# A Nyström attention and MLP kernel: 64x32 products for C·v, ScalarE's squares for the row deviations, landmark sums exchanged by DMA, and a new order of work

## The chip, the cores and the metric

The kernel runs on one core of one Trainium2 chip. The metric is the device time of one execution in microseconds, as the median of several runs. Beside it stands one profiled execution, from which all durations of parts are taken; its own time is told by its span, from the first to the last instruction.

## What is computed

Inputs q, k, v are (8 batches, 8 heads, 576 rows, 64 columns). For each batch and head the rows are averaged in 32 groups of 18 into landmarks, three softmaxes are formed, one 32x32 matrix is inverted by six steps of an iteration, and the product goes, batch by batch, into a layer norm and a two-layer MLP with a residual.

```python
q_lm = q.reshape(B, H, 32, 18, D).mean(axis=3)      # k_lm alike
A = sm(q, k_lm); Bm = sm(q_lm, k_lm); C = sm(q_lm, k)
Z = Bm^T / (norm1(Bm) * norminf(Bm) + 1e-6)
for _ in range(6): Z = 2 * Z - Z @ Bm @ Z
x = (A @ Z @ C @ v)  as rows of 512 = 8 heads x 64
out = x + relu(layernorm(x) * g @ w1) @ w2          # w1 512x2048, w2 2048x512
```

## The kernel before

**Units and sets.** A unit is four heads of one batch, so that a batch has two units. Batch 0 goes first by a path of its own; batches 1, (2, 3), (4, 5), (6, 7) are the sets 0 to 3 of `def_set`, and in a set of four units the units go in pairs y = 0, 1. The name of a tile ends in the set and the pair or unit.

**An order written out.** Every step is declared with `op(name, engines, tiles, function)`. The string `ORDER` lists all steps by number with the letter of the engine that does each (P TensorE, D VectorE, A ScalarE, G GpSimd, S the SyncE queue, which only issues DMAs). Each engine works through its own steps strictly in that order; across engines only the data decide. A tile takes the first free slot of its kind (`slots`, lines 297 to 305), and waits for the slot's last reader.

**Landmark sums** (lines 694 to 763). The rows of a head lie nine to a partition, so that the 18 rows of a landmark are two neighbouring groups of nine, in two places of the transposed unit `xT`. For k VectorE reduces `xT` (`add_`, two reductions of 128x576 per unit, 24 in all); for q GpSimd adds the nine rows in four steps (`asum_`), VectorE transposes and reduces the small rest (`sT_`, `sR_`). Both leave in `part` the sums of one half of the heads' landmarks on one block of 32 partitions and of the other half on the next block. `spread` (line 796) is two matmuls with the constant matrix `spread16`, which bring both halves to all blocks in PSUM (`psp`), and `lm` (line 802) copies them to SBUF. From `lm` come three products: `psb` (scores of landmarks with landmarks), `psec` (landmarks of q with k) and `psea` (landmarks of k with q).

**Tile places.** TensorE's array is used in parts where the operands are small: `tile_position=(rb, cb)` gives the first row and column of the part. `psb`, `psec`, `psea` and the iteration use 32x32 parts, of which 16 exist; `psec` as written uses eight (its column place is `32 * ((p_ + 2 * (w % 2)) % 4)`, the same for r = 0 and r = 1), `psea` all sixteen. `product` (line 876), C times v, uses 64x64 parts: 18 groups of four matmuls for a pair of products, each with 64 landmarks of two heads and 130 columns, which are v's columns and a column of ones of both heads. Half of what it gives is one head's landmarks with the other head's v, and is not used.

**v's load.** `load_into` (line 320) brings a unit of v by one DMA, `load_swapped` (line 323) by three, since the heads then have to lie in other partitions.

**Layer norm and MLP.** `rows` makes 128 rows of x in PSUM (`psy`), `x_` copies them to SBUF on ScalarE or VectorE (line 983), `measure` (line 996) takes mean and variance on VectorE by bn_stats and bn_aggr, 36 times, and `rstd` turns five or four blocks' variances into 1/deviation on ScalarE. `psm`, `psh`, `relu` (ScalarE and VectorE) make the hidden layer; `pso` or, for batches 2 to 7, the seven products `ps7a`, `ps7c`, `ps7e` of `def_seven` with its `hmix` sums (GpSimd and VectorE) the second; results are added to x on VectorE and stored by DMAs from SP and ScalarE.

Of the kernel before, what the change touches and what calls it, by code (L numbers as in the profile page):

```python
# [10 lines left out]
FP32 = mybir.dt.float32  # L11
UINT32 = mybir.dt.uint32
# [4 lines left out]
P = 128  # L17

ORDER = """
0G 20P 23P 4S 12P 14P 24P 17P 11P 2S 1S 3S 6S 7S 10P 21P 28G 38P 25A 26D 34P 39D 40P 29P 30A 31P 27D  # L20
37P 32P 42D 41D 18P 33D 43P 65P 44A 45D 66A 61P 67P 46P 47P 250G 48D 22P 19P 15P 62A 68A 69A 71D
245G 49P 50D 63P 35P 13P 79G 80D 51P 52D 64A 36A 81P 70D 53P 72P 73A 5S 95S 54D 8P 9D 105A 106G 55P
56D 57P 74P 82D 260P 83D 58D 16P 84D 96S 59P 75A 76A 60D 85P 251D 86D 89P 90D 87P 88D 126P 261A 262D
108G 77G 94S 103G 93S 97S 101G 91D 92D 78D 107A 102G 127P 128P 129P 130A 167P 141P 142A 252P 253A
145P 169D 104A 168D 98S 254D 149P 150D 147P 148A 172P 173A 176P 247P 177A 248A 259D 255D 174P 175A
246D 256P 257A 146A 170P 171D 109G 110G 121P 122P 123P 111G 124P 268P 156P 258D 151D 249D 267P 112A
125A 275A 269A 270A 271A 157D 277A 158D 131P 132P 133P 134P 178P 163P 278D 279D 117G 273A 433G 274A
99S 113G 135A 180D 263S 164A 159P 280P 281D 160A 165P 166A 114G 264A 100S 115G 116G 265S 118G 136P
137P 266G 161P 179D 429G 119G 138P 139P 162D 282P 283D 140A 181P 182A 183P 284P 276D 285A 143P 187P
184D 286P 144A 188A 272D 152D 185P 186A 287D 297P 298D 299D 189P 191D 190D 288P 289A 294P 290P 295A  # L30
201P 202P 296A 300P 301A 291D 292P 293A 120G 455G 212P 213P 435G 436G 437G 310P 438G 445G 302A 303G
308P 309A 214P 330P 434D 444D 312D 311D 313D 332D 192P 193A 153D 154D 198P 199A 155A 441D 430D 439D
431D 331D 442D 440D 432D 443D 234P 556D 215P 304P 235P 236P 305A 306A 196P 446G 447G 203P 204P 194P
195A 237P 238P 205P 206P 451G 197A 307G 314P 315A 337P 339P 448G 449D 822G 338A 555D 239P 240P 241P
322P 207P 208P 574D 565D 569G 450D 340A 323A 216P 242D 209D 210S 217P 324D 341P 343D 223P 335P 244S
336A 342D 333P 463D 218P 219P 577G 452D 220D 344P 352P 353D 467G 468G 469G 470G 334A 826G 348P 345A
349A 346P 347A 457G 318P 319A 224P 316P 317A 225P 226P 227P 481P 458G 465D 459G 460G 482A 350P 454D
354D 357P 471D 464D 472D 351A 453D 363P 228P 229P 364D 358A 361P 230P 362A 461D 462D 365D 493P 494A
359P 368P 360A 483P 495P 355P 325D 326D 505A 369A 356A 231D 233A 200G 374P 375P 366P 367A 370P 371A
573G 506D 456D 507P 508P 509D 320P 321D 385P 484P 486A 487A 489A 510P 834D 511D 466D 491A 386P 387P  # L40
485A 388P 211S 512P 376P 473S 474G 490A 377P 496P 498A 501A 499A 497A 513D 514P 327D 488D 492D 328D
396P 397P 475S 476G 566G 828G 829G 830G 831G 572G 477S 478G 838G 839G 844G 564G 568G 503A 378P 379P
380P 515D 823D 502A 221S 504D 372P 516P 479S 480A 500D 517D 836D 528P 529P 530D 531D 398P 399P 373A
# [57 lines left out]
1496D 1521D 1427D 1523P 1524P 1525P 1421S 1526P 1428A 1516G 1515G 1522D 1529P 1530P 1429A 1531P  # L101
1532P 1527D 1528D 1539P 1540P 1564P 1541P 1542P 1168S 1533D 1535S 1418A 1536D 1537A 1538S 1543D
1534S 1545S 1432A 1546D 1548A 1547A 1549P 1565P 1550P 1566P 1551P 1567P 1568D 1569S 1570S 1552P
1553P 1554P 1555P 1544A 1556P 1557D 1558A 1559S
"""


# [1156 lines left out]
```

## Time and profile before

| what | value |
|---|---|
| median of 3 runs (lowest, highest) | 260.67 us (260.29, 261.9) |
| span of the profiled execution | 258.5 us |
| TensorE busy | 249.9 us, 97% of the span, 3499 matmuls |
| VectorE busy | 212.3 us, 82%, 472 instructions |
| ScalarE busy | 163.9 us, 63%, 304 instructions |
| GpSimd busy | 177.5 us, 69%, 180 instructions |
| DMA | 36.3 MB, mean 140 GB/s |

The profile names an instruction by its line, engine, operation and tiles, written out<-in with buffer numbers left out. PE is TensorE's matmul, PEld its weight load, DVE VectorE, ACT ScalarE, POOL GpSimd, SP the queue that issues DMAs; a trailing q marks an engine's sequencer. Matmuls overlap one another, so the mean duration of one is longer than the time it adds; the chain of waits cuts the time into pieces without overlap and is the better scale for a group. In the chain's rows stand the start, the length, the engine with the output tile, and xN, the number of instructions of the piece.

### The profile page before, as it was taken

What the parts mean: (1) busy time and instruction counts of PE and PEld (TensorE: products, weight loads), DVE (VectorE), ACT (ScalarE), POOL (GpSimd) and SP (SyncE); (2) the same over time, 40 slices, a digit from 0 to 9 for tenths busy, and PEclk for the clock granted to TensorE, in tenths of its full rate; (3) what the DMA queues carried; (4) which work ended last, traced back from release to release, by engine and by line L of the source; (5) the groups of instructions that cost most, each with busy time, mean ns of one, the idle gap of its engine ahead of it and who ended that gap; (6) DMA issues with size and microseconds to landing.
All of it is one profiled execution on the core that took longest, in us unless ns stands there. A gap on an engine that the chain in (4) does not pass through costs nothing.

```text
span 258.5 us, 8351 instructions
## 1 busy us (share of the span) xinstructions
PE 249.9 (97%) x3499; PEld 179.8 (70%) x3499; DVE 212.3 (82%) x472; ACT 163.9 (63%) x304; POOL 177.5 (69%) x180
## 2 busy tenths in 40 slices
PE   7898999999999999999999999999999999999993
PEld 7766465556554557777766787777867787788981
DVE  1669899999999989997998869898547999878661
ACT  1588886747766999778756997868666245644000
POOL 8324899689794789699999995782078505966600
PEclk9999999999999999999999999999999999999999
DMA  6999999999749176949704832500130100510356
GB/s 234 367 269 338 374 210 208 207 235 244 227 127 178 29 164 87 221 89 286 140 4 121 231 93 61 127 3 3 41 85 0 44 20 9 115 23 20 82 121 184
DMA packets 23277, 36.32 MB, mean 140 GB/s; under 512 B 2116, under 2 KB 11592, under 8 KB 23240
## 3 DMA queue, kind: packets, MB, share of 16 engines
q1 hardware_dynamic: 12456, 23.37, 29.6%
q0 software_dynamic: 9504, 10.36, 25.1%
q10 hardware_dynamic: 1280, 2.07, 3.1%
q8 instruction: 27, 0.44, 0.7%
q14 instruction: 10, 0.08, 0.1%
HBM read 36.70 MB, written 9.44 MB: 178 GB/s over the span
## 4 chain that ended last, share of the span: by engine, by line
PE 85%; DMA 7%; ACT 3%; DVE 2%; issue 1%; SPq 1%; ACTq 0%; DVEq 0%
PE psh L193 23%; PE ps7a L193 16%; PE pso L193 15%; PE ps7c L193 8%; DMA w1s<-in_moe_w_ch_dram 5%; PE ps7e L193 4%; PE psm L193 3%; PE psy L193 3%; DMA stg_q<-in_q_dram 3%; PE it L193 2%; PE pscv L193 2%; PE psd L193 1%; PE psec L193 1%; PE psea L193 1%; PE pso_74a L193 1%
## 5 line engine op out<-in xcount | busy, mean ns | idle before, releaser
L203 ACT ACTIVATE hT<-psh 128x576 f16<-128x576 f32 x106 | 65.8, 650 | 30.4 <-PE psh L193 28.6
L193 PEld LDWEIGHTS <-hT 128*128 128x128 f16 x688 | 64.6, 98 | 22.6 <-issue 3.1
L193 PE MATMUL psh<-ea,m 128*128 128x288 f16 x512 | 78.2, 286 | 0.1
L193 PEld LDWEIGHTS <-m 128*128 128x128 f16 x512 | 48.9, 98 | 15.6 <-issue 1.3
L193 PE MATMUL pso<-w,hT 128*128 128x512 f16 x176 | 45.5, 380 | 0.0
L207 POOL TENSOR_TENSOR mix<-hT 128x1024 f16<-128x1024 f16 x8 | 17.0, 2125 | 27.4 <-ACT hT L203 27.4
L210 DVE SCALAR_TENSOR_TENSOR x<-ps7a,rstd,x 128x256 f32<-128x256 f32 x48 | 21.3, 477 | 6.7 <-PE ps7a L193 4.9
L193 PE MATMUL ps7a<-mix,hT 128*128 128x256 f16 x192 | 25.9, 273 | 0.0
L1068 DVE TENSOR_SCALAR hT<-psh 128x576 f16<-128x576 f32 x22 | 16.4, 753 | 10.1 <-PE psh L193 9.9
L997 DVE BATCH_NORM_STATS2 six<-x 128x6 f32<-128x512 f32 x36 | 24.2, 673 | 0.0
L207 POOL TENSOR_TENSOR ea<-ea,lns 128x576 f16<-128x576 f16 (+1 forms) x14 | 17.7, 1261 | 7.2 <-ACT lns L203 4.0
L200 ACT CAST m<-psm 128x512 f16<-128x512 f32 (+1 forms) x25 | 19.1, 793 | 4.5 <-PE psm L193 3.4
L200 ACT COPY x<-psy 128x512 f32<-128x512 f32 (+1 forms) x29 | 16.8, 587 | 7.6 <-PE psy L193 7.2
L193 PEld LDWEIGHTS <-mix 128*128 128x128 f16 x192 | 18.2, 98 | 4.3 <-issue 1.5
L207 POOL TENSOR_TENSOR mix<-mix,hT 128x1024 f16<-128x1024 f16 x8 | 16.9, 2124 | 6.2 <-DVE mix L207 5.8
L207 POOL TENSOR_TENSOR hT<-hT 128x1024 f16<-128x1024 f16 x9 | 19.1, 2123 | 0.2
L207 POOL TENSOR_TENSOR hT<-hT,mix 128x1024 f16<-128x1024 f16 x7 | 15.1, 2166 | 4.4 <-PE ps7e L193 2.5
L214 DVE TENSOR_REDUCE part<-xT_k 128x32 f16<-128x576 f16 x24 | 17.1, 737 | 0.0
L207 POOL TENSOR_TENSOR asum_q<-asum_q 128x256 f32<-128x256 f32 (+1 forms) x24 | 15.1, 628 | 1.5
L203 ACT ACTIVATE ec<-psec 128x256 f16<-128x256 f32 (+1 forms) x42 | 12.4, 428 | 5.3 <-PE psec L193 5.3
L193 PE MATMUL psy<-zcbd,ea 128*128 128x256 f16 x80 | 14.8, 273 | 0.2 <-ACT x L200 0.2
L200 POOL CAST natv<-stg_v 128x1152 f16<-128x1152 f32 (+1 forms) x12 | 13.8, 1163 | 1.4 <-DMA stg_v<-in_v_dram 1.3
(174 smaller groups left out, 471.2 us busy)
## 6 DMA issues: line engine op xcount, KB each, us to landing
out_dram<-x SPq DMA_DIRECT2D x55, 128.0 KB, 2.7
stg_v<-in_v_dram SPq DMA_DIRECT2D x10, 576.0 KB, 5.1
w1s<-in_moe_w_ch_dram SPq DMA_DIRECT2D x8, 512.0 KB, 11.6
nat_q<-in_q_dram POOLq DMA_DIRECT2D x7, 576.0 KB, 8.7
nat_k<-in_k_dram POOLq DMA_DIRECT2D x7, 576.0 KB, 7.5
w<-in_moe_w_ch_dram POOLq DMA_DIRECT2D x4, 512.0 KB, 8.5
out_dram<-x ACTq DMA_DIRECT2D x15, 128.0 KB, 2.4
stg_v<-in_v_dram SPq DMA_DIRECT2D x6, 288.0 KB, 4.5
```

The source lines that it names most:

```text
L193: keep(nc.tensor.matmul(o, l, r, start=start, stop=stop, tile_position=(rb, cb), skip_group_check=(skip or cb != 0)))
L200: keep(nc.scalar.copy(o, i) if e == "A" else ENGINES[e].tensor_copy(out=o, in_=i))
L203: keep(nc.scalar.activation(*args, **kw))
L207: keep(ENGINES[e].tensor_tensor(out=o, in0=a, in1=b, op=f))
L210: keep(ENGINES[e].scalar_tensor_tensor(out=o, in0=a, scalar=s, in1=b, op0=f0, op1=f1))
L214: keep(nc.vector.tensor_reduce(out=o, in_=i, axis=axis, op=f))
L997: keep(nc.vector.bn_stats(out=T(f"six_{j}")[:], in_=T(f"x_{j}")[:]))
L1068: keep(nc.vector.tensor_scalar(out=o, in0=T(psh)[:, :, 0:HS], scalar1=0.0, scalar2=None, op0=ALU.max))
```

## The change

Six things change together.

1. **64x32 products.** `product` makes, instead of one matmul with 64 landmarks and 130 columns, two with 32 landmarks and 65 columns of their own head's v. There are twice as many matmuls (288 become 576), in eight places of 64x32; the results and what reads them (`cv`) are half as wide.
2. **ScalarE's squares.** `x_` also gives the row sum (`accum_out`), and `measure` becomes one ScalarE Square of 128x512 per block, with the row sum as bias and the sum of squares as a second output. bn_stats and bn_aggr go.
3. **Landmark sums by DMA.** `spread16`, the two matmuls `psp` and the copy `lm` go. The reductions write the middle of three places of `lm`, and `spread` is four DMAs, SBUF to SBUF, that bring the neighbouring block's half into the first or third place. Six pairs, 24 DMAs, all given to SP.
4. **Sixteen places.** `psec` moves its column place with r in sets 1 to 3.
5. **v's second slot in pieces.** `load_crossed` lays heads into other halves and quarters of the partitions, by five DMAs for an even unit of sets 1 to 3 and six for an odd one, where one and three stood.
6. **A new order** of all steps with engines chosen anew. By the letters in the two tables: relu 106 on ScalarE and 22 on VectorE become 93 and 35; x_ 29 and 11 become 24 and 16; hmix 32 on GpSimd and 16 on VectorE become 26 and 22; norm 14 on GpSimd and 4 on VectorE become 18 and none; casts 12 on GpSimd become 14; w1's scaling 12 on GpSimd and 4 on ScalarE become 10 and 2, with 4 on VectorE; stores 58 on SP, 16 on ScalarE become 44, 27 and three on GpSimd.

```diff
+    def copy_summed(e, o, i, total):
+        if e == "A":
+            act(o, i, AF.Copy, accum_out=total)
+        else:
+            keep(nc.vector.tensor_scalar(out=o, in0=i, scalar1=1.0, scalar2=0.0, op0=ALU.mult, op1=ALU.add,
+                                         accum_out=total))
...
-    def load_swapped(t, src, b, u, e):
+    def load_crossed(t, src, b, u, e, odd):
         heads = src[b, 4 * u:4 * u + 4].rearrange("h (t j) d -> h t j d", j=NJ)
-        dma(e, t[:, 0, :, :], heads[1:3].rearrange("h t j d -> (h t) j d"))
+        if not odd:
+            dma(e, t[:, 0, :, :], heads[0:2].rearrange("h t j d -> (h t) j d"))
         for i in range(2):
-            dma(e, t[ts(1 - i, 64), 1, :, :], heads[3 * i])
+            if odd:
+                dma(e, t[ts(1 - i, 64), 0, :, :], heads[i])
+            at = 64 * (i ^ odd)
+            for z in range(2):
+                dma(e, t[ds(at + 32 * (1 - z), 32), 1, :, :], heads[2 + i, ds(32 * z, 32)])
...
-                buf(f"part_{s}{y}", "part", [P, 2, 2, 2, LM // 2, 2], FP16)
+                buf(f"lm_{s}{y}", "lm", [P, 2, 2, 2, 3, LM // 2, 2], FP16)
...
-                def spread(e, ps=ps, part=part):
-                    for half in range(2):
-                        MM(T(ps)[:, half, :, :].rearrange("p k c -> p (k c)"),
-                           spread16[:, half, :, :, :].rearrange("p e a w -> p (e a w)"),
-                           T(part)[:].rearrange("p n w r l x -> p (n w r l x)"))
-                op(f"spread_{s}{y}", "P", (ps, part), spread)
-                op(f"lm_{s}{y}", "AD", (ps, lmn),
-                   lambda e, ps=ps, lmn=lmn: copy(e, T(lmn)[:].rearrange("p k h c -> p h k c"), T(ps)[:]))
+                def spread(e, lmn=lmn):
+                    for p_ in range(4):
+                        dma(e, T(lmn)[ts(p_, 32), :, :, :, 2 - 2 * (p_ % 2)].rearrange("p n w r l x -> p (n w r) (l x)"),
+                            T(lmn)[ts(p_ ^ 1, 32), :, :, :, 1].rearrange("p n w r l x -> p (n w r) (l x)"))
+                op(f"spread_{s}{y}", "SA", (lmn,), spread)
...
-                                cb = 32 * ((p_ + 2 * (w % 2)) % 4)
+                                cb = 32 * (p_ ^ (2 * (w % 2)) ^ (r if swaps else 0))
...
-                            rows, cb = ts(half, 64), 64 * (half ^ x)
-                            MM(T(pscv)[ds(cb, 64), x, ts(y, D2)], T(f"ecT_{s}{w}")[rows, j // 2, :, j % 2],
-                               natv_of[b][rows, u, j, :, :].rearrange("p r e -> p (r e)"),
-                               rb=64 * half, cb=cb, start=(j == 0), stop=(j == NJ - 1), skip=True)
+                            for r in range(2):
+                                rows, cb = ts(half, 64), 64 * (half ^ x) + 32 * r
+                                MM(T(pscv)[ds(cb, 32), x, ts(y, D + 1)],
+                                   T(f"ecT_{s}{w}")[rows, j // 2, ds(32 * r, 32), j % 2],
+                                   natv_of[b][rows, u, j, r, :],
+                                   rb=64 * half, cb=cb, start=(j == 0), stop=(j == NJ - 1), skip=True)
...
             def measure(e, u=u, j=j):
-                keep(nc.vector.bn_stats(out=T(f"six_{j}")[:], in_=T(f"x_{j}")[:]))
-                keep(nc.vector.bn_aggr(out=T(f"stats_{b}")[:, u, :], in_=T(f"six_{j}")[:]))
-            op(f"measure_{j}", "D", (f"x_{j}", f"six_{j}", f"stats_{b}"), measure)
+                act(squares[:], T(f"x_{j}")[:], AF.Square, bias=T(f"stats_{b}")[:, u, 0:1], scale=-float(DM),
+                    accum_out=T(f"stats_{b}")[:, u, 1:2])
+            op(f"measure_{j}", "A", (f"x_{j}", f"stats_{b}"), measure)
```

**TensorE at the landmark scores of set 3.** Names: `psp` is the spread's output, `psh` and the `ps7` tiles are the MLP, `psec` and `it<-lm` the products of landmarks. Before:

```order
L193 LDWEIGHTS spread_72
L193 MATMUL psp<-part,spread_72 128x256
L193 LDWEIGHTS m
L193 MATMUL psh<-ea,m 128x288
...
L193 LDWEIGHTS hT
L193 MATMUL ps7a<-mix,hT 128x256
```

After:

```order
L192 LDWEIGHTS hT
L192 MATMUL ps7c<-w_16_79,hT 128x256
L192 LDWEIGHTS lm
L192 MATMUL psec<-xT_k,lm 32x288
...
L192 MATMUL it<-lm 32x32
```

The spread's matmuls stood among the MLP's; now the first instruction of the set that needs the sums, `psec`, stands right behind an MLP product, and `it<-lm` of both pairs follows it directly.

**VectorE at the end of set 1's sums.** `part` or `lm` is what the reductions write, `six` and `stats` are bn_stats' and bn_aggr's, `rsum` opens the softmax of the landmark scores. Before:

```order
L214 TENSOR_REDUCE part_1473<-sT_q_1523 128x64
L210 SCALAR_TENSOR_TENSOR m_1512<-less_998,zsum_1228,psm_1499 128x512
L997 BN_STATS six_1581<-x_1461 128x6
L998 BN_AGGR stats_1368<-six_1581 128x2
L997 BN_STATS six_1584<-x_1454 128x6
L998 BN_AGGR stats_1368<-six_1584 128x2
L210 SCALAR_TENSOR_TENSOR x_802<-pso_1383,rstd_1253,x_802 128x512
L214 TENSOR_REDUCE rsum_1613<-it_1543 128x4
```

After:

```order
L220 TENSOR_REDUCE lm_1553<-sT_q_1574 128x2x32
L216 SCALAR_TENSOR_TENSOR x_816<-pso_1209,rstd_1377,x_816 128x512
L213 TENSOR_TENSOR w1_16_78<-w1_16_78,less_728 128x2x512
L206 CAST natv0_76<-stg_v_1612 128x2x9x64
L220 TENSOR_REDUCE rsum_1724<-it_1634 128x4
```

The two pairs of bn instructions are gone from between the last sum and the softmax; one correction of w1 and one cast of v came in their place.

**SP in the same stretch.** Before, from the first stores on:

```order
L223 DMA out_0_dram<-x_718 64x512
L223 DMA stg_v_1740<-in_v_dram 128x2x576
L223 DMA stg_v_1819<-in_v_dram 128x576
L223 DMA stg_v_1819<-in_v_dram 64x576 x2
L223 DMA stg_v_1832<-in_v_dram 128x2x576
L223 DMA out_0_dram<-x_1030 64x512
```

After:

```order
L229 DMA stg_v_1518<-in_v_dram 32x576 x2
L229 DMA out_0_dram<-x_1019 64x512
L229 DMA stg_v_1612<-in_v_dram 128x576
L229 DMA stg_v_1612<-in_v_dram 32x576 x4
L229 DMA lm_1553<-lm_1553 32x8x32 x4
L229 DMA stg_v_1761<-in_v_dram 64x576
```

The four DMAs of the second pair's sums stand on SP behind a store and behind a unit of v in five pieces, and the next unit's six pieces follow them.

253 lines of the change are left out of this document (123 added, 130 removed), and 2 rows, old and new, of the table w2_src.

## The prediction, made before the changed kernel was run

> **What bounds the kernel now.** I read the page's busy shares first, then the busy times by stage, then who TensorE itself waited for, and last the chain that ended last.
>
> ```profile
> PE 249.9 (97%) x3499; PEld 179.8 (70%) x3499; DVE 212.3 (82%) x472; ACT 163.9 (63%) x304; POOL 177.5 (69%) x180
> PEclk9999999999999999999999999999999999999999
> PE 85%; DMA 7%; ACT 3%; DVE 2%; issue 1%; SPq 1%; ACTq 0%; DVEq 0%
> ```
>
> ```profile
> 36.00:60.00 24.00, 23.83 (x255) 13.22 (x254) 23.63 (x49) 15.18 (x30) 20.43 (x26) 1.00 1.19 224
> 60.00:100.00 40.00, 40.00 (x631) 22.99 (x630) 37.67 (x80) 30.90 (x60) 32.01 (x37) 1.00 0.70 151
> 100.00:150.00 50.00, 49.90 (x790) 36.81 (x788) 45.45 (x102) 38.17 (x73) 46.61 (x41) 1.00 0.64 151
> 150.00:190.00 40.00, 40.00 (x721) 30.54 (x719) 30.37 (x75) 30.76 (x60) 22.24 (x14) 1.00 0.21 50
> 190.00:254.00 64.00, 64.00 (x589) 52.18 (x587) 49.49 (x98) 24.78 (x43) 35.19 (x18) 1.00 0.23 58
> ```
>
> ```profile
> PE idle L193 <- DVE zeros L252: 1.4, 1, 1.4
> PE it L193 <- DVE st L210: 0.4, 1, 0.4
> ```
>
> The columns of the stages are length, then busy time (and instructions) of TensorE, its weight loads, VectorE, ScalarE, GpSimd. From 36 us to 254 us TensorE is busy 217.7 of 218 us, at the full clock, and its longest wait for anyone after the first one is 0.4 us. So there the time is the sum of what TensorE is given, and an instruction taken from it is time won at once. The other engines matter only if one of them makes it wait. VectorE is the nearest to that: 98% busy from 36 to 60, 94% and 91% in the next two stages, 76% and 77% after 150 us. The first 36 us hang on loads.
>
> ```profile
> 15.84 11.95 DMA w1s<-in_moe_w_ch_dram
> ```
>
> That is the chain's longest wait, and the change keeps these bytes; I give the start no gain, and 1.5 us either way for its new order.
>
> **What TensorE loses and gains.** Pieces of the chain on the same scale, without overlap:
>
> ```profile
> 37.12 0.75 PE pscv L193 x34
> 110.24 0.56 PE psm L193 x16
> 170.49 1.18 PE pscv L193 x70
> 171.90 0.34 PE psm L193 x8
> ```
>
> ```profile
> 65.23 0.30 PE it L193 x32
> 104.62 0.63 PE psec L193 x30
> 173.66 0.43 PE psea L193 x31
> 60.60 0.22 PE psp L193 x2
> ```
>
> (The counts fall a little short where records are missing or a neighbour overlaps; two products are 72 matmuls, one scores block 32.)
>
> *64x32 products.* `psm` is the row for this shape: 64x32 parts, eight places, 512 columns. Eight cost 0.34 us, sixteen 0.56, so a second round of eight adds 0.22 us, that is 0.43 ns per column with all eight at work, and 0.12 us of either piece is getting in and out of the shape. The present product has 18 rounds of four: (1.18 − 0.12) / 18 = 59 ns, where 130 columns by 0.43 ns are 56 ns. It is bound by its columns. With 65 columns and eight places the columns take 28 ns a round. The shortest rounds in the trace, the 32 landmark scores in eight rounds of four (0.30 − 0.12 us), take 23 ns, so nothing shorter is in the way. Best case: 18 × 28 = 0.50, with 0.12 makes 0.62 us, 0.56 won per 72. Worst case: matmuls start no faster than in the scores, 0.31 us for 32 or 9.7 ns each; 144 of them take 1.40 + 0.12 = 1.52 us, 0.34 lost. I take 35 ns a round, since the nearest row, `psm`, shows eight places at work without a surcharge: 0.75 us, 0.43 won. There are 288 / 72 = 4 such portions: **−1.7 us**, between −2.2 and +1.4.
>
> The Trainium skill's "TensorE: Matmul & The Clock Gate", section "Measured speedup vs the span model", speaks against it: a pack takes the duration of one matmul plus about 4 ns for each further tile. By that a round would go from 56 + 12 to 28 + 28 ns, an estimate of 0.2 us won in all instead of 1.7, and a total of about 258.3 us. The second `psm` round cost the columns alone, with no 28 ns on top, so this trace does not bear it out for rounds that follow one another.
>
> *Sixteen places.* `psec` and `psea` are 32 matmuls of 288 columns each; what differs is that `psea`'s second half takes the other eight places. 0.63 against 0.43: 0.20 us in six blocks, **−1.2 us**, between −1.3 and 0. *The spread's matmuls* go: 6 × 0.22 = **−1.3 us**.
>
> Together −4.2 us.
>
> **What moves between the other engines.**
>
> ```profile
> L997 DVE BATCH_NORM_STATS2 six<-x 128x6 f32<-128x512 f32 x36 | 24.2, 673 | 0.0
> L998 DVE BATCH_NORM_AGGREGATE stats<-six 128x2 f32<-128x6 f32 x36 | 6.6, 182 | 1.2
> L1068 DVE TENSOR_SCALAR hT<-psh 128x576 f16<-128x576 f32 x22 | 16.4, 753 | 10.1 <-PE psh L193 9.9
> L200 DVE COPY x<-psy 128x512 f32<-128x512 f32 x8 | 5.5, 682 | 0.0
> L207 DVE TENSOR_TENSOR hT<-hT,mix 128x1024 f16<-128x1024 f16 x5 | 4.3, 870 | 0.0
> ```
>
> ```profile
> L203 ACT ACTIVATE hT<-psh 128x576 f16<-128x576 f32 x106 | 65.8, 650 | 30.4 <-PE psh L193 28.6
> L203 ACT ACTIVATE lns<-lns 128x576 f32<-128x576 f32 x16 | 10.9, 683 | 0.4
> L203 ACT ACTIVATE w<-w1s,g_sb 128x512 f16<-128x512 f32 x4 | 2.9, 720 | 0.9 <-DMA w1s<-in_moe_w_ch_dram 0.9
> L200 ACT COPY x<-psy 128x512 f32<-128x512 f32 x24 | 13.9, 588 | 6.7 <-PE psy L193 6.4
> ```
>
> VectorE loses 36 × 0.855 = 30.8 us of statistics, and takes 13 relus (9.8), five x copies (3.4) and six hidden mixes (at 0.87: 5.2): about 12 us less in all. ScalarE gets 36 squares. The trace has no square and no second output; the nearest rows read SBUF as well, 683 ns for 576 columns (607 for 512) and 720 ns, so 0.6 to 0.72 us and some room above for the sum: 25 us at 0.7. It gives up 13 relus (8.5), five copies (2.9), four `lm` copies (2.3), and two scalings (1.4), and ends some 10 us higher, near 174 of 255. Both lie beside TensorE's work: nothing for either. If that cover went, a late relu would hold `psh`, which has two slots in PSUM; ScalarE's waits for `psh`, 28.6 us in the row above, are what it has to give first.
>
> **The landmark sums by DMA.** This is the wait that is added.
>
> ```profile
> L223 SPq DMA_DIRECT2D out_dram<-x x58: 466/588/994, 53.8 to 254.8; - x58
> DMA to landing us min/median/max: 2.1/2.5/6.8
> SPq L223 <- DVE x L210: 146.4, 16, 30.9
> ```
>
> ```profile
> L200 ACT CAST lm<-psp x4: 580/585/585, 60.9 to 152.7; 128x512 f16<-128x512 f32 x4
> 36.00:60.00 24.00, 3.37 (x8) 1.00 1.19 224
> 60.00:100.00 40.00, 5.06 (x12) 1.00 0.70 151
> 100.00:150.00 50.00, 5.75 (x14) 1.00 0.64 151
> ```
>
> Before, the way from the last reduction to the first scores was 0.22 us of matmuls, 0.58 of copy and the hand-overs, some 1.2 us. Now it is four issues in a row on SP, 0.59 us each (the trace has no DMA from SBUF to SBUF; a store of a block is the nearest, 466 to 994 ns), and 2.5 us from the last issue to its landing: 4.9 us, 3.7 later. What is late next is `psec` or `it<-lm` on TensorE, and behind it everything TensorE has in its order, since it takes nothing out of turn. The cover is that the sums themselves come sooner. Of the statistics (the last three rows are the busy time of bn_stats and bn_aggr by stage) 14.2 us lay between 36 and 150 us, before the last set's sums, on an engine that was 91 to 98% busy; against that stands about half of the 18 us that VectorE takes over. That is some 5 us sooner, a little more than 3.7. So I put down **+0.3 us**, between 0 and 14, the price without cover that the first rival works out.
>
> SP gets 66 pieces of v where 24 stood, 24 sums, and 14 stores fewer: 52 issues more, 31 us of its time. A unit of v in six pieces is 3.5 us in which what stands behind it, the sums among it, waits. SP spends 146 us waiting for blocks to store, so in sum it has the time; the bytes are the same. ScalarE's eleven further stores are issued by its sequencer in that engine's order. None of this has a price on TensorE beyond the 0.3.
>
> **The sum.** 258.5 − 1.7 − 1.2 − 1.3 + 0.3 = 254.6 us of span. The median of the runs shown lies 260.67 − 258.5 = 2.2 us above the profiled span, so the forecast is **256.8 us**, 1.5% faster. About 1%, 2.6 us, is what a measurement of this kernel can tell from no change, so faster means below 258.1 and slower above 263.3.
>
> **Rivals.**
>
> *The sums hold TensorE* (slower). For it: the order puts `psec` of set 3 right behind an MLP product and `it<-lm` behind that, so the stretch between last reduction and first use, which the spread's place among `psh` products filled before, is empty; and SP may be in the middle of a unit of v. Against it: VectorE's relief. Mechanism: TensorE stands at the first scores of each of the three sets until four issues and a landing are over, once for each pair. At 3.7 us less 0.6 for what lies between, for three sets: +9.3, and half again for the second pairs, +14: 258.5 − 4.2 + 14 + 2.2 = 270.5 us. It decides from (4.2 + 2.6) / 6 = 1.1 us per pair on; below (4.2 − 2.6) / 6 = 0.27 us it leaves the forecast faster.
>
> *The products pay nothing* (same). If places in one row of the array start one after another, the product costs 1.4 more instead of 1.7 less: 259.9 us. For it: twice the instructions, and no run of more than 72 small matmuls in the trace. Against it: `psm`.
>
> *ScalarE becomes late* (same). From 60 to 190 us it is already 76 to 77% busy, and the squares come on top of relus, on which `psh` waits. If two dozen of the 93 relus come 0.12 us late each, 2.9 us go: 259.7 us. Against it: each relu has the time of two `psh` steps.
>
> *The start shortens too* (faster). w1's first load no longer waits for a slot behind v, and TensorE reaches its full stretch 2 us sooner: 254.8 us. Against it: DMA is the limit there and the bytes are the same.
>
> *The sixteen places change nothing*, because starts stay in order: 258.0 us, faster by a hair; `psea` has the same loops and is shorter, which speaks against it.
>
> **Chances.** Forecast 0.50; start shortens 0.12; places nothing 0.06; products pay nothing 0.12; ScalarE late 0.09; sums hold TensorE 0.11. Of the forecast's 0.50 about 0.06 falls above 258.1, and half of the places' 0.06: faster 0.44 + 0.12 + 0.03 = 0.59, slower 0.11, the same 0.30. The range of 8 in 10 runs from the start's rival less half its own 1.5 us of play, 254.0, to 262.0, which takes in the dead products and a late ScalarE and the mild end of the held sums.
>
> **What would show it.** Right: two products near 0.75 us in the chain where 1.18 stood; `psec` blocks near 0.43; no `psp`; TensorE still busy without a gap from 36 us on; `lm` DMAs landing before TensorE's previous MLP product ends. Wrong: idle time of TensorE or its weight loads ahead of `psec` or `it<-lm` put down to a DMA of `lm`; product rounds above 59 ns; TensorE's stretch with gaps behind a relu; an end of the first loads later than now.

## The result, and the profile after

The changed kernel takes **310.53 us** (median of 4 runs, 308.16 to 311.85) where the kernel before took 260.48 in the same measurement: a ratio of 1.190, 95% interval 1.185 to 1.196. It is 50 us slower; 256.8 was forecast. The profiled execution spans 306.4 us, at a mean granted clock of 0.952 (before: 1.000). Ratios here and below leave out runs that are more than 1.5% above the fastest of the same kernel, so one can lie below the ratio of the medians beside it.

Busy shares, clock by slices and the chain's shares, of the page of the changed kernel:

```profile
PE 261.7 (85%) x3775; PEld 181.7 (59%) x3775; DVE 218.1 (71%) x440; ACT 174.4 (57%) x371; POOL 171.2 (56%) x177
PEclk9966999979889999999897999799999999999998
PE 56%; DVE 25%; DMA 9%; issue 5%; ACT 1%; SPq 1%; POOL 1%; DVEq 0%
```

TensorE was 97% busy and 85% of the chain; now it is 85% busy and 56% of the chain, a quarter of which is VectorE. TensorE's busy time has risen by 12 us although it was given fewer columns; parts of its work ran at a lower clock. The same stages as before (length, then busy time of TensorE, its weight loads, VectorE, ScalarE, GpSimd; then the clock):

```profile
36.00:60.00 24.00, 21.47 (x282) 12.42 (x281) 21.46 (x41) 18.84 (x40) 19.91 (x24) 1.00 1.09 183
60.00:100.00 40.00, 31.60 (x539) 16.92 (x539) 30.51 (x58) 20.49 (x50) 21.55 (x27) 0.91 0.70 132
100.00:150.00 50.00, 43.94 (x556) 28.73 (x555) 45.57 (x83) 33.68 (x67) 34.91 (x35) 0.97 0.64 135
150.00:190.00 40.00, 35.12 (x573) 24.67 (x571) 29.11 (x65) 27.22 (x56) 26.16 (x22) 0.96 0.29 71
190.00:254.00 64.00, 60.21 (x943) 45.71 (x944) 43.42 (x89) 42.41 (x91) 29.84 (x17) 0.97 0.18 46
```

No stage is gapless any more. Whom TensorE waited for (us in total, times, longest):

```profile
PE ps7a L192 <- DVE x L216: 6.9, 9, 1.3
PE psm L192 <- DVE x L216: 4.9, 1, 4.9
PE it L192 <- DMA lm<-lm: 4.0, 1, 4.0
PE pscv L192 <- issue: 3.7, 2, 2.2
PE psl_q L192 <- DMA nat_q<-in_q_dram: 3.5, 1, 3.5
PE ps7a L192 <- DVE hT L213: 3.3, 1, 3.3
PE it L192 <- issue: 1.7, 1, 1.7
PE psec L192 <- DMA lm<-lm: 1.7, 5, 0.4
```

Three kinds stand here: VectorE late, landmark sums late (`lm`), and "issue", in which TensorE waits for nothing that the profile shows. The last is new in kind: it falls into the doubled products. The chain (start, length) around one of them:

```profile
156.65 1.27 PE pscv L192 x142
157.91 2.25 issue
160.16 0.21 PE pscv L192 x2
```

And VectorE's wait of 4.9 us begins with one instruction, in a timeline of VectorE and GpSimd:

```profile
52.86 5.77 DVE L213 TENSOR_TENSOR w<-w,less 128x1024 f16<-128x1024 f16 x1
53.47 1.29 POOL L213 TENSOR_TENSOR ea<-ea,lns 128x576 f16<-128x576 f16 x1
54.70 1.16 POOL L206 CAST natv<-stg_v 128x1152 f16<-128x1152 f32 x1
55.82 2.25 POOL L213 TENSOR_TENSOR mix<-w 128x512 f16<-128x512 f16 x2
```

A correction of w1 that took 0.82 us on the mean before took 5.77 here; GpSimd started work beside it 0.6 us after its start and paused 0.6 us before its end.

### The profile page after: what moved, and what is told of

Same layout as the page of the kernel before. It is cut to its first block, busy times and chain, and to the rows that moved or that the text cites. A ratio compares the mean times of both kernels' runs of the same rounds, so it can differ in the third digit from the quotient of the medians.

```text
span 306.4 us, 9047 instructions
## 1 busy us (share of the span) xinstructions
PE 261.7 (85%) x3775; PEld 181.7 (59%) x3775; DVE 218.1 (71%) x440; ACT 174.4 (57%) x371; POOL 171.2 (56%) x177
## 4 chain that ended last, share of the span: by engine, by line
PE 56%; DVE 25%; DMA 9%; issue 5%; ACT 1%; SPq 1%; POOL 1%; DVEq 0%
PE psh L192 14%; PE ps7a L192 12%; PE pso L192 9%; DVE x L216 5%; PE ps7c L192 4%; DMA nat_q<-in_q_dram 4%; DMA lm<-lm 4%; DVE lm L220 3%; PE ps7e L192 3%; DVE hT L213 3%; PE it L192 3%; PE psm L192 2%; PE psy L192 2%; DVE m L216 2%; DVE mix L213 2%
## 5 line engine op out<-in xcount | busy, mean ns | idle before, releaser
L209 ACT ACTIVATE hT<-psh 128x576 f16<-128x576 f32 x93 | 58.3, 648 | 44.7 <-PE psh L192 42.0
L192 PE MATMUL psh<-ea,m 128*128 128x288 f16 x512 | 81.6, 293 | 0.9 <-DVE m L216 0.5
L1074 DVE TENSOR_SCALAR hT<-psh 128x576 f16<-128x576 f32 x35 | 26.2, 750 | 6.8 <-PE psh L192 6.4
L209 ACT ACTIVATE squares<-x,stats 128x512 uint8<-128x512 f32 x36 | 25.9, 719 | 0.4
L213 POOL TENSOR_TENSOR mix<-hT 128x1024 f16<-128x1024 f16 x6 | 12.7, 2125 | 22.7 <-DVE hT L1074 10.8
L206 ACT CAST m<-psm 128x512 f16<-128x512 f32 (+1 forms) x25 | 17.4, 725 | 8.3 <-PE psh L192 4.7
L209 ACT ACTIVATE ec<-psec 128x256 f16<-128x256 f32 (+1 forms) x42 | 12.8, 427 | 9.1 <-PE psec L192 9.1
L209 ACT ACTIVATE x<-psy 128x512 f32<-128x512 f32 (+1 forms) x24 | 14.3, 595 | 6.1 <-DMA out_dram<-x 3.8
L220 DVE TENSOR_REDUCE lm<-xT_k 128x32 f16<-128x576 f16 x24 | 17.3, 731 | 0.0
L209 ACT ACTIVATE lns<-psd 128x576 f32<-128x576 f32 x16 | 10.4, 651 | 10.9 <-PE psd L192 10.6
L192 PE MATMUL psm<-w,zt 64*32 64x512 f16 x256 | 12.1, 397 | 4.9 <-DVE x L216 4.9
L192 PE MATMUL ps7a<-w,hT 128*128 128x256 f16 x96 | 13.4, 273 | 3.2 <-DVE x L216 3.2
```

What stands on the lines that cost most here:

```text
L192: keep(nc.tensor.matmul(o, l, r, start=start, stop=stop, tile_position=(rb, cb), skip_group_check=(skip or cb != 0)))
L206: keep(nc.scalar.copy(o, i) if e == "A" else ENGINES[e].tensor_copy(out=o, in_=i))
L209: keep(nc.scalar.activation(*args, **kw))
L213: keep(ENGINES[e].tensor_tensor(out=o, in0=a, in1=b, op=f))
L220: keep(nc.vector.tensor_reduce(out=o, in_=i, axis=axis, op=f))
L1074: keep(nc.vector.tensor_scalar(out=o, in0=T(psh)[:, :, 0:HS], scalar1=0.0, scalar2=None, op0=ALU.max))
```

## The experiments

The starting theories. **A**: a run of many short matmuls empties TensorE's instruction supply, and VectorE's long fp16 adds are held up by GpSimd in the new order. **B**: the edits themselves cost the 50 us, whatever the order. The kernel before was run beside each group; it took 260.35 to 260.58 us.

### The edits in the old order

The code of the changed kernel, with the table of the kernel before: same sequence and engines, `spread` on SP where its matmuls stood, `lm` dropped, `measure` on ScalarE.

> All edits of the change (64x32 products, squares on ScalarE, landmark sums by DMA, sixteen places, v in pieces), but the operations in the order and on the engines of the kernel before; each sum's DMA stands where the spread's matmuls stood, on SP. Theory A (the new order lets VectorE's long fp16 adds and subtractions run beside GpSimd, and VectorE becomes late): these adds go back to about 0.8 us from 1.23, and the time falls to 258 to 270 us, the rest being products that stall for instructions (some 6 us) and sums that TensorE waits for. Theory B (the edits themselves cost the 50 us, whatever the order): 295 us or more.

Measured: 293.98 us, ratio 1.130 (1.127 to 1.132), just short of theory B's number and far from A's: the edits cost 33.5 us without any new order, and the new order 16.5 more. One part of A did come: VectorE's long adds took 0.84 us on the mean here, as against 1.23 in the new order. The runs that follow take the two parts in turn.

### The products

*Alone*, in the old order:

```
-  MM(T(pscv)[ds(cb, 64), x, ts(y, D2)], T(f"ecT_{s}{w}")[rows, j // 2, :, j % 2],
-     natv_of[b][rows, u, j, :, :].rearrange("p r e -> p (r e)"), ...)
+  for r in range(2):
+      MM(T(pscv)[ds(cb + 32 * r, 32), x, ts(y, D + 1)],
+         T(f"ecT_{s}{w}")[rows, j // 2, ds(32 * r, 32), j % 2],
+         natv_of[b][rows, u, j, r ^ (1 if swapped(w) and half == x else 0), :], ...)
```

> The kernel before with one edit, the 64x32 products, in its own order. Theory A (instruction supply): gaps put down to issue of 1 to 2 us appear in each of the three later products, and the time is 3 to 5 us above the kernel before, near 264. Rival, the prediction's term: 1.7 us less, 258.8. Second rival (starts bind): no stall, 1 us more or less.

Measured: median 277.09 us (273.4 to 278.1), ratio 1.056 (1.052 to 1.060). One edit that was to win 1.7 us loses 14 to 17. The profiled execution is one of the longer, 277.6 us at a mean clock of 0.968; the shortest had 0.987. TensorE's waits:

```profile
PE pscv L193 <- issue: 7.0, 3, 4.4
PE it L193 <- issue: 2.6, 1, 2.6
```

The longest, and the product in front of it, in the timeline:

```profile
79.90 1.30 PE L193 MATMUL pscv<-natv,ecT 64*32 64x65 f16 x138
85.57 0.25 PE L193 MATMUL pscv<-natv,ecT 64*32 64x65 f16 x6 [4.37 <-issue]
```

And the clock behind it (the column after the brackets of GpSimd):

```profile
82.00:84.00 2.00, 0.00 (x0) 0.00 (x0) 0.00 (x0) 0.00 (x0) 0.00 (x0) 1.00 1.18 195
84.00:86.00 2.00, 0.43 (x7) 0.25 (x8) 0.12 (x1) 0.00 (x0) 0.00 (x0) 0.57 1.21 205
86.00:88.00 2.00, 2.00 (x6) 0.61 (x4) 0.65 (x3) 0.00 (x0) 0.00 (x0) 0.50 0.15 28
88.00:90.00 2.00, 2.00 (x52) 0.97 (x51) 1.26 (x3) 0.73 (x2) 0.00 (x0) 0.50 0.00 0
90.00:92.00 2.00, 2.00 (x23) 0.72 (x22) 1.67 (x4) 0.65 (x2) 0.00 (x0) 0.72 0.02 4
```

So this stall is paid twice: 4.4 us of standing, and 6.8 us at half the clock (0.43 + 0.50 + 0.50 + 0.28 of two microseconds each lost, 3.4 us), of which the first 1.3 us still fall into the standstill. The four stalls, 2.6, 4.4, 0.9 and 1.8 us, make 9.7; the half clock after three of them costs about 8 more (there was none after the 0.9); 9.7 + 8 is near the 17.4 us by which the span grew (275.9 to 258.5).

What is waited for shows in the trace's DMA records. TensorE's instructions come in packets of 16,384 bytes, about one for every 256 matmuls and weight loads (29 packets here, 27 before). Each stall ends 2.3 to 2.5 us after the start of such a packet, and each comes after an instruction whose number, counted in TensorE's order, differs from the others' by a multiple of 256:

```
packet starts         19.98   83.08  140.05  183.14 us
stall ends            22.26   85.57  142.41  185.58 us
stands after number     705    2497    4289    5825
```

The stalls put down to "issue" in the changed kernel come after the last three of these numbers too. A pair of products is now 288 instructions in 1.2 us. TensorE passed the mark 256 before a stall at 79.93, 140.30 and 182.54 us (the last three stalls). The packets at 140.05 and 183.14 started within 0.6 us of that, with the DMA engines nearly idle; the one at 83.08 started 3.15 us later, with the DMA engines full (a share of 1.18 in the window above). In the kernel before, the product was 144 instructions in the same 1.2 us, and long matmuls followed; a packet that started at 80.66 us held up nothing.

*Two-column matmuls beside the old products*: the number of instructions without the new form. (The output is then not the reference's.)

```
   MM(T(pscv)[ds(cb, 64), x, ts(y, D2)], T(f"ecT_{s}{w}")[rows, j // 2, :, j % 2], ...)
+  MM(T(pscv)[ds(cb, 64), x, ds(400, 2)], T(f"ecT_{s}{w}")[rows, j // 2, :, j % 2],
+     natv_of[b][rows, u, j, 0, 0:2], ...)
```

> The kernel before with its own products, and behind each of their matmuls one of two columns into unused space, so that the number of TensorE's instructions is that of the 64x32 products in the old form. Theory A (the instruction supply): gaps put down to issue of 1 to 4.5 us at the same places, a lower clock behind the longer ones, 270 to 278 us. Rival (the 64x32 form is what stalls): no gap over 0.5 us there, 261 to 264 us.

Measured: 275.71 us, ratio 1.057 (1.051 to 1.062).

```profile
PE pscv L193 <- issue: 6.2, 3, 4.0
PE it L193 <- issue: 2.7, 1, 2.7
```

The same four stalls, after the same four instruction numbers. It is the number of instructions, not the 64x32 form. The half clock shows here as well: 3.4 us of it after the stall of 2.7 us, 6.8 us with the one of 4.0, none after those of 1.4 and 0.8.

*Half the products*: 64x64 places with 65 columns, 72 matmuls, once in the changed kernel and once in the old order. The second slot's heads get the first slot's values.

```
-  for r in range(2):
-      MM(T(pscv)[ds(cb + 32 * r, 32), ...], T(f"ecT_{s}{w}")[rows, j // 2, ds(32 * r, 32), j % 2], ...)
+  for r in range(1):
+      MM(T(pscv)[ds(cb, 64), ...], T(f"ecT_{s}{w}")[rows, j // 2, :, j % 2], ...)
```

> The changed kernel with 64x64 places and 65 columns in the landmark-value products: half the matmuls (72 instead of 144), the heads of the second slot get the values of the first, so this part is left out. Theory A (a run of 288 short matmuls outruns the instruction supply): the gaps of 1.4, 2.3 and 1.7 us put down to issue within and behind the products go, and the time falls by 5 to 7 us, to about 304. Rival (they come from the order or the trace): gaps of that size stay, and the time falls by less than 2 us.

> The kernel before with 64x64 places and 65 columns in the products: as many matmuls as before, with half the columns; the heads of the second slot get the values of the first, so this part is left out. Theory A (the columns were a cost, the number of instructions is the other): 72 matmuls take 0.7 us instead of 1.18, no stall, 1.9 us less: 258.6 us. Rival (a matmul cannot start sooner whatever its columns): 1.1 us as before, 260.5 us.

Measured: 302.99 us in the changed kernel, 7.5 less, with the stalls gone; 259.17 in the old order, ratio 0.995 (0.994 to 0.997), two of its three pairs in 0.71 us where 1.18 stood, all without a stall. So the columns were a cost that could be won, as the prediction said, where the number of instructions stayed the same.

*The products cut in pieces* of 40 and 32 matmuls, with MLP matmuls between them (in set 3 the two middle pieces stand together):

```
-  product_20 product_21 rcv_2 cv_2 pso_12_04 pso_12_06 pso_10_14
+  product_20a pso_12_04 product_20b pso_12_06 product_21a pso_10_14 product_21b rcv_2 cv_2
```

> The kernel before with the 64x32 products alone, as in the run of that edit, but the three later pairs of products are cut in pieces of 40 and 32 matmuls, with two to four wide MLP matmuls between the pieces. Theory A (288 instructions in 1.2 us empty what TensorE's instruction supply holds, and the next 256 can be used only some 2.4 us after their transfer begins): the gaps of 4.4, 1.8 and 0.9 us put down to issue shrink to under 0.5 us each, the clock keeps 1.00 behind them, and the time falls from 277 to 262 to 267 us. Rival (many short matmuls cost this wherever they stand): the gaps add up to about the same, and the time stays above 273 us.

Measured: 278.02 us, ratio 1.067 (1.065 to 1.068): no gain, against theory A's number.

```profile
PE pscv L193 <- issue: 3.0, 2, 2.7
PE psm L193 <- DVE cv L207: 2.3, 1, 2.3
```

The stalls of 0.9 and 1.8 us have shrunk to 0.3 in all in sets 2 and 3. In set 1 it is still 2.7, since its packet again starts late, at 82.72 us, with the DMA engines full; and in set 3 `psm` now waits 2.3 us for `cv`, because the MLP products that covered VectorE's step stand between the pieces. The mean clock is 0.969, as low as before (0.968). One wait was exchanged for another.

### The squares

*Alone*, in the old order, with `measure` on ScalarE and the copies of x summing:

```
-  bn_stats(six, x); bn_aggr(stats[:, u, :], six)
+  act(squares, x, Square, bias=stats[:, u, 0:1], scale=-DM, accum_out=stats[:, u, 1:2])
```

> The kernel before with one edit, the sums and squares of x on ScalarE instead of the statistics on VectorE, in its own order and with every other operation on its old engine. The prediction's reading (both lie beside TensorE's work): 260 us, the same. Theory C (ScalarE, 33 us more where it was at 76 to 77%, makes psh wait): TensorE waits for relus by 4 us or more in sum and its clock falls behind them: 265 to 272 us.

Measured: 273.27 us, ratio 1.049 (1.047 to 1.051), just above theory C's numbers. (The edit also takes one of the four slots of `s16`, a small tile of the landmark sums, as the changed kernel does; no run takes that apart.)

```profile
PE 252.8 (93%) x3499; PEld 179.7 (66%) x3499; DVE 185.6 (68%) x411; ACT 192.3 (71%) x405; POOL 177.4 (65%) x180
```

That is the page's row of busy shares; TensorE's waits:

```profile
PE psh L194 <- ACT hT L211: 3.2, 4, 1.1
PE psd L194 <- ACT hT L211: 1.8, 2, 1.5
PE psec L194 <- ACT hT L211: 0.9, 1, 0.9
```

VectorE lost 27 us of work and ScalarE gained 28; neither is busy for more than 71% of the span, and still TensorE waits about a microsecond at a time; half of it, 6 us, is for relus of the engine that now has 36 squares between them, the rest for other work of both engines. These are theory C's waits. Its loss of clock did not come: no wait is longer than 1.5 us, and the mean clock is 0.996.

*With 41 operations moved to even the engines out*: every fourth relu and every second copy of x to VectorE, at the place where it stood.

```
-  338A   (relu_102)
+  338D
```

> The kernel before with the squares on ScalarE, and every fourth relu and every second copy of x moved from ScalarE to VectorE (41 operations), in the old order. Theory C (273 us came from ScalarE having 197 us of work, and relus late): TensorE's waits for relus go back to under 2 us, 261 to 264 us. Rival (operations put on another engine at the place where they stand come late whichever engine it is, since each engine takes its work in order): TensorE then waits for VectorE as well, 267 us or more.

Measured: 290.43 us, ratio 1.115 (1.113 to 1.117): 17 us worse, with ScalarE back at 170 us and VectorE at 213.

```profile
PE psh L194 <- DVE m L208: 2.9, 2, 1.6
PE psh L194 <- DVE hT L1080: 2.8, 4, 1.0
PE ps7a L194 <- DVE x L218: 2.7, 5, 0.8
PE psh L194 <- ACT hT L211: 1.9, 3, 0.8
```

Theory C fell in its simple form. VectorE has as much work as in the kernel before (212.3 us) and is waited for all the same: what counts is what stands ahead of an operation in its engine's order when TensorE needs it.

### The sums and the places

*The sums by DMA together with the products*, each DMA where the spread's matmuls stood:

```
-  MM(psp, spread16, part) x2; copy(lm, psp)
+  four DMAs lm[.., the other half's] <- lm[.., own half's], on SP
```

> The kernel before with two edits, the 64x32 products and the landmark sums by DMA, in its own order, each sum's DMA where the spread's matmuls stood. Against the run with the products alone (277 us), the prediction's terms (+0.3 for the wait, -1.3 for the matmuls): 276 us. Theory D (TensorE stands at each set's first scores until four issues and a landing are over, 1 to 4 us per set, and loses clock behind the longer ones): 280 to 290 us, with waits of TensorE put down to lm.

Measured: 278.25 us, ratio 1.064 (1.059 to 1.069), some 1 to 2 us above the products alone.

```profile
PE it L193 <- DMA lm<-lm: 2.8, 6, 0.5
PE psec L193 <- DMA lm<-lm: 1.0, 1, 1.0
```

TensorE waits 3.8 us for the sums, mostly in pieces of half a microsecond (four DMAs, one after the other), less the 1.3 us of matmuls saved. The time lies between the prediction's terms (276) and theory D (280 or more). The products' own stalls fell to 7.8 us in this run, so its distance to the products alone is not the price of the sums by itself. The clock is also less simple here: it stayed at 1.00 after stalls of 2.0 and 1.8 us, and was 0.50 for 3.4 us after four waits of under 0.6 us each (69 to 72 us).

*The sixteen places*, with the loads of v in pieces:

```
-  cb = 32 * ((p_ + 2 * (w % 2)) % 4)
+  cb = 32 * (p_ ^ (2 * (w % 2)) ^ (r if swaps else 0))
```

> The kernel before with one edit, the scores of k on sixteen places, with the loads of v in pieces that it needs. The prediction's term: 1.2 us less, 259.2 us, psec blocks near 0.43 us. Rival (the pieces cost more than the places win: 52 issues on SP come between other loads and stores, and casts of v come late): TensorE waits for a cast of v or its load, and the time is 262 us or more.

Measured: 260.61 us, ratio 1.000 (0.998 to 1.002). From the first `psec` of a pair to what follows it, in the timeline before and with this edit:

```profile
68.97 0.70 PE L193 MATMUL psec<-xT_k,lm 32*32 32x288 f16 x32
69.49 0.28 PE L193 MATMUL it<-st 32*32 32x64 f16 x16
```

```profile
69.86 0.50 PE L193 MATMUL psec<-xT_k,lm 32*32 32x288 f16 x32
70.19 0.38 PE L193 MATMUL it<-st 32*32 32x64 f16 x16
```

From the one line's start to the other's it is 0.52 us before and 0.33 now, and 0.19 to 0.21 less in five of the six blocks (0.10 in the sixth): the term is real. It does not show in the median. In the profiled execution the first relu starts 1.3 us later than before and the last one 0.4 us later, so 0.9 us were won between them and the start took them away; why the start was longer is open. The loads of v in pieces, which this run also has, may be the reason; no run has the places without them.

### The new order

*VectorE's adds in another form*, in the changed kernel:

```
+  if e == "D" and f in (ALU.add, ALU.subtract):
+      return stt(o, a, 1.0, b, ALU.mult, f)
```

> The changed kernel, with VectorE's fp16 tensor_tensor additions and subtractions written as scalar_tensor_tensor (times 1.0, then add or subtract): the same result and the same sizes. Theory A (a 128x1024 tensor_tensor gives way to GpSimd: 0.68 us alone, 2.3 us beside it): the other form takes some 1.2 us whether GpSimd works or not, the sum of these 30 instructions stays near 36 us, but none is longer than 1.5 us; TensorE's waits of 5.0 and 3.7 us for VectorE go, and 8 to 20 us of the time: 290 to 302 us. Rival (the stretch comes from DMA traffic or from a wait within VectorE): the other form is stretched as well, to 2 us and more, and the time stays at 305 us or more.

Measured: 316.32 us, ratio 1.215 (1.213 to 1.217). The stretch stays with the other form. By GpSimd's busy time beside each of the 30 instructions: in the changed kernel 19 with GpSimd idle take 0.68 us and 10 with GpSimd busy for at least half of them 2.3; in this form 17 take 1.21 and 10 take 2.7, the longest 7.1. None of those beside an idle GpSimd takes longer than 0.69 and 1.23 us. So theory A's expectation that another form escapes was wrong; that GpSimd is what stretches them is borne out. Instructions of VectorE with one input in PSUM show none of it: the 84 updates of x, 128x256, take 0.48 us beside GpSimd and without. The Trainium skill's "SBUF — State Buffer", section "Who interferes with whom", says this: a VectorE instruction with two SBUF inputs contends with GpSimd instructions that read SBUF. The trace agrees, 0.68 against 2.3 us.

*GpSimd's adds left out* (a fill with zeros instead):

```
+  if e == "G" and f in (ALU.add, ALU.subtract) and o.dtype == FP16:
+      return keep(nc.gpsimd.memset(o, 0.0))
```

> The changed kernel with GpSimd's fp16 additions and subtractions left out (a fill with zeros in the same places instead), so the output is not the reference's. Theory A (VectorE's long adds give way to GpSimd, and in the new order they stand beside each other): the 30 adds of VectorE fall from 1.23 us to about 0.7 us, TensorE's waits of 15.7 and 4.6 us for VectorE shrink by more than half, and the time falls by 12 to 22 us, to 289 to 299. Rival (VectorE has too much to do in the new order, or the stretch has another cause): the adds stay above 1 us on the mean, or the time stays above 304 us.

Measured: 307.93 us (304.3 to 308.0), ratio 1.179 (1.172 to 1.186), against theory A's 289 to 299. VectorE's adds fall from 1.23 to 0.95 us (casts and sums of GpSimd still stand beside some), yet only 2.6 us are won: TensorE's gaps (starts of matmuls over 0.25 us later than usual for their kind, each put down to what released it) behind VectorE's x and hT fall from 20.3 to 14.0 us, those behind lm rise from 7.5 to 9.7, and the clock falls to 0.942.

*VectorE's adds left out* instead, in the changed kernel:

```
+  if e == "D" and f in (ALU.add, ALU.subtract) and o.dtype == FP16:
+      return keep(nc.vector.memset(o, 0.0))
```

> The changed kernel with VectorE's fp16 additions and subtractions left out (a fill with zeros in the same places), so the output is not the reference's. Theory E (in the new order VectorE's work is what arrives last, so each of its microseconds in the stages before 150 us counts): VectorE loses some 27 us, TensorE's waits for x, hT and m of VectorE go below 8 us in sum, and the time falls by 12 to 20 us, to 290 to 298, the level of the edits in the old order. Rival F (something else, such as the sums' way through SP or the products' stalls, takes the place of each wait): above 303 us.

Measured: 298.17 us, ratio 1.144 (1.143 to 1.146): 12.4 us for 20.7 us of VectorE's work. Theory E, if just outside its numbers: in the new order much of VectorE's work arrives last, and more than half of each microsecond taken from it counts. (The fill also drops the add's waits for its inputs, and the old order was not run with the same fill.)

*The old engines in the new sequence.* In the changed kernel 105 relus, casts, copies and mixes go back to the engines that the kernel before gave them:

> The changed kernel, in its new sequence, but relus, casts of m, copies of x, mixes and hidden mixes on the engines that the kernel before gave them (105 operations), so that VectorE has 13 relus and six long adds fewer. Theory E1 (the share of work between the engines makes VectorE late): 290 to 300 us. Rival (the sequence itself makes the waits): 305 us or more; with ScalarE's squares and its old relus together TensorE then waits for ScalarE in VectorE's place.

Measured: 323.60 us, ratio 1.238 (1.231 to 1.245). Worse, so the old engines do not repair the new sequence. With much the same engines the old sequence took 293.98, so the sequence has a price of its own, some 30 us with these engines.

*The sums' 24 DMAs issued by ScalarE*, one letter in the table for each `spread`:

```
-  481S 492S ...
+  481A 492A ...
```

> The changed kernel with the landmark sums' 24 DMAs issued by ScalarE instead of SP, at the same places of the order. Theory G (the sums wait behind SP's pieces of v and stores): TensorE's waits for lm, 7.5 us in sum, fall to 4 us or less, and the time falls by 3 to 8 us. Rival (they wait for VectorE's last reductions and for their own landing): the waits stay above 6 us, or the time within 2 us of 310.

Measured: 316.84 us, ratio 1.217 (1.213 to 1.221). Theory G's gain did not come: the gaps put down to lm grew to 10.5 us. The chain of the changed kernel shows what stood before such a wait:

```profile
74.03 1.49 DVE lm L220 x3
...
76.26 6.40 DMA lm<-lm
```

The window within that last step has the DMA engines full (a share of 1.18):

```profile
78.00:80.00 2.00, 0.34 (x17) 0.17 (x16) 0.00 (x0) 0.00 (x0) 0.00 (x0) 1.00 1.18 232
```

So the scores wait for VectorE's last reductions and, behind an update of x that is left out here, for the sums' own way of 6.4 us; the median way of the 24 DMAs is 2.5. With ScalarE as issuer, the chain at this place has

```profile
81.10 2.71 DMA lm<-lm
```

So this landing did become shorter. But the four issues now stand in ScalarE's order among its relus, and the chain from 68 to 86 us has ScalarE's queue (19%), relus (16%), squares (8%) ahead of the scores. The other queue moved the wait rather than took it away.

## Why the prediction was wrong, step by step

**The bound was read rightly.** "The time is the sum of what TensorE is given" held: half the products' columns, in as many matmuls, won 1.2 us (ratio 0.995). But it is a statement about the kernel before, whose order left TensorE no wait; the products, the squares and the sums each made some.

**The products, −1.7 us: this is the first step that failed.** "Nothing shorter is in the way" was taken from `psm`, a run of 16 matmuls, and from 32 scores. In the run with the products alone the first 32 matmuls of a product start within 0.13 to 0.15 us, 32 to 37 ns a round of eight where I took 35; from the 33rd on they start 8.3 ns apart, 66 ns a round:

```
matmul of the product    1st   33rd   73rd  137th
starts (79.9 us +)      0.00   0.23   0.56   1.09 us
```

144 of them take about 1.2 us, as long as the 72 before (1.18). So even without a stall the term would have been nothing. The estimate set beside the term, 56 ns a round, was nearer to the 66 than the 35 taken; by its own figures (68 to 56 ns in 72 rounds) it wins 0.9 us and not the 0.2 written there. The stalls and the lower clock behind them, 14 to 17 us, were in no term, and in none of my bounds, +1.4 at worst. The rival "the products pay nothing" had the direction, and a tenth of the price; I noted for it that no run of more than 72 small matmuls stood in the trace, and then did not widen the range by it.

**The other engines, "nothing for either": the second step that failed.** Squares alone cost 12.8 us. I compared busy sums with the span, and they stayed below it. What hides work is not a sum but the slack of each operation at its place in an order that each engine keeps. The rival "ScalarE becomes late" assumed 0.12 us for two dozen relus, 2.9 us; the waits were about 1 us each. The sum itself came out: in the changed kernel ScalarE ends at 174.4 us, where 174 was forecast, in part by luck, since a square was dearer than the 0.7 us taken and some casts left the engine:

```profile
L209 ACT ACTIVATE squares<-x,stats 128x512 uint8<-128x512 f32 x36 | 25.9, 719 | 0.4
L209 ACT ACTIVATION_READ_ACCUMULATOR squares<-x,stats 128x1 f32 x36 | 6.9, 192 | 0.0
L209 ACT ACTIVATION_READ_ACCUMULATOR x<-psy 128x1 f32 (+1 forms) x24 | 4.9, 203 | 0.0
```

Each sum is read out by an instruction of its own, 12 us of them in all, of which some 4 lie outside ScalarE's other work.

**VectorE's durations, carried over.** I priced hidden mixes at 0.87 us. In the new order the same instructions take:

```profile
L213 DVE TENSOR_TENSOR w<-w,less 128x1024 f16<-128x1024 f16 x8 | 12.6, 1589 | 0.0
L213 DVE TENSOR_TENSOR mix<-mix,hT 128x1024 f16<-128x1024 f16 x7 | 8.6, 1221 | 0.0
```

Before, w's took 0.82, and every add beside an idle GpSimd 0.65 to 0.69. The thirty adds of 128x1024 took 36.6 us where 24 had taken 18.6: 18 us more, and 5.2 were priced. That is most of why VectorE did not end 12 us lower but 6 us higher (218.1 against 212.3). The mean of 0.87 with a best case of 0.68 was a sign that I passed over. How the new order's own part, 16.5 us, divides is open. VectorE's lateness is in it, since 12.4 us go when all of its adds go; but only 2.6 go with GpSimd's adds, which take 8 us of the stretch with them, and the sequence with the old engines is slower still. Each wait that was taken away was followed by another.

**The sums by DMA, +0.3 us.** The mechanism and the first rival's place were right (TensorE at `it<-lm` and `psec`); the size in the old order is 3.8 us of waits for 1.3 us saved, in the new order 7.5 us of gaps. Issue (0.61 us) and median landing (2.5) were as priced; the longest landing, 6.7, met full DMA engines. The cover that I counted on, VectorE's relief, did not come. The rival's 14 us were not reached; the slower side came from elsewhere.

**The sixteen places, −1.2 us**: right, 0.2 us in five of six blocks, and smaller than what moves the start of one execution.

**The clock** was in no term. It was 1.00 throughout before, where TensorE had no wait over 0.4 us after its start; in these runs most pauses of 2 us and more came with a stretch of 3.4 us or more at half the clock. The length of one pause does not decide it: in the run with products and sums a pause of 2.0 us cost no clock, and four short waits close together did.

No version tried here that computes everything beats the kernel before; the places alone are equal to it.

## What to carry to other kernels

A kernel whose bottleneck has no gaps is a fine balance: price an edit there by the slack of each operation in its engine's own order, not by busy sums, and allow for what the clock can lose around pauses of some 2 us, here up to 3.4 us for one. Halving the columns of matmuls by doubling their number won nothing here, where a run is longer than some 32, and a run of 288 instructions in 1.2 us had to stop for the next packet of instructions. A shape's price holds only for runs as long as the one it was read from.

## What the runs showed of the hardware

- TensorE's instructions arrive in packets of 256; the next was used about 2.4 us after its transfer started, and where the DMA engines were full a transfer started 3.15 us late (stalls of 0.9, 1.8, 2.6 and 4.4 us, all at multiples of 256 instructions from one another). The Trainium skill's "Runtime: NRT & Kernel Launch", section "Instruction fetch mechanics", has the blocks of 256 and calls the cost of crossing one mostly hidden; the size agrees, and what is hidden depends on the pace, as 288 instructions in 1.2 us show.
- Of a run of 64x32 matmuls the first 32 start within 0.13 to 0.15 us, the rest 8.3 ns apart; cut in pieces with wide matmuls between, each piece's first 32 are fast again (0.13 us).
- Around standstills of 1.8, 2.6 and 4.4 us the granted clock was 0.50 for 6.8, 3.4 and 6.8 us; after 0.9 us it stayed at 1.00 (the products alone). After 1.8 and 2.0 us in the run with products and sums it stayed at 1.00 too.
- VectorE's fp16 add of two SBUF tiles took 0.68 us with GpSimd idle and up to 5.8 us beside it.
